# A spectral filter's second step, taken for two groups at a time on the four quarters of the matrix array

## The chip, the cores and the metric

The kernel runs on one core of a Trainium2 chip. The metric is the time of one execution on the device in microseconds (us). A core has TensorE (PE in the profile, with PEld for the loading of its weights), VectorE (DVE), ScalarE (ACT), GpSimd (POOL), SyncE (SP) and 16 DMA engines. Each engine takes its instructions in the order in which they are written; engines wait for each other through semaphores. Matmuls read SBUF and write PSUM, which DVE and ACT read; here POOL works on SBUF.

## The reference

Two layers, each a spectral filter A and then a token MLP B, both on a normalised input and added to it. x is 2048 x 640 in float32.

```python
def _A_ref(x, w_r, w_i):
    X = jnp.fft.rfft2(x, axes=(-2, -1))
    X = X * (w_r + 1j * w_i)
    return jnp.fft.irfft2(X, s=(S, D), axes=(-2, -1))

def _B_ref(x, w1, b1, w2, b2):
    h = _layernorm(x, axis=-1)
    u = _gelu(jnp.einsum("bsd,sf->bdf", h, w1) + b1)
    y = jnp.einsum("bdf,fs->bds", u, w2) + b2
    return y.transpose(0, 2, 1)

for layer in range(2):
    x = x + _A_ref(_layernorm(x), A_w_r, A_w_i)
    x = x + _B_ref(_layernorm(x), B_w1, B_b1, B_w2, B_b2)
```

## The kernel before

Transforms are matmuls with constant tables. To keep float32's precision at the speed of f16, an operand is split into a high and a low f16 part (names ending in h and l), and a product is three matmuls: high by high, high by low, low by high. The split is made by two engines: ACT writes the high part, DVE (or POOL) the rest.

The order of the program is `run` (L1371): in layer 1 it normalises, folds and takes the first matmul step over the 2048 rows, whose results are s1h and s1l; then `a1` (L408), the filter stage, which this case is about; `a2` (L675), the inverse's last steps; and the MLP (`b1st` L847, `b2nd` L1072), which runs `a1` and `a2` of layer 2 in between. `a1` sets `self.pin` (L574): from there each engine's order is the order of the text, through the helper at L48 that records nearly every operation. So the profile shows nearly everything at L49, and groups are told by their tiles.

`a1` works on 16 groups of the spectrum. One group passes through these steps:

- D, `dstage` (L481): 16 matmuls of 160 or 161 columns, the step over the 640 channels, from s1h, s1l, tables tD and a stacked rest (stk, by DMA through DRAM).
- ph and pl, `psplit` (L494): the split of D's result, 128 x 642, on ACT and DVE.
- S, `s2stage` (L517): the second step over rows, 12 matmuls of 128x128 weights (table tS2, half of it zeros) and 321 columns.
- ta and tb, `product` (L555): DVE multiplies S's result in PSUM by the filter's real and imaginary parts w (321 KB by DMA a group); POOL forms the complex product by two operations of 128 x 321.
- xh and xl, `xsplit` (L503), with the group's scale sx; `twice` (L511) copies 126 columns of each, on ACT and POOL.
- I, `is2stage` (L541): the inverse of S, 36 matmuls of 64x128 weights and 128 columns, two row halves at a time.
- Y, yt, Y2h, Y2l: `yevict` (L432) and `y2evict` (L447) on ACT read I's result; `y2split` (L452) on POOL casts yt to Y2h and forms the rest Y2l.

The loop (L584 to L632) runs these shifted: in the round of group g, PE runs D of g+1, I of g-3 and S of g; DVE takes ta and tb of g-1, pl of g+1, xl of g-2; ACT takes ph of g+1, xh of g-2, Y and yt of g-3. PSUM is a ring of four tiles of two banks, `big` (L89), used in the order of D, I, S. Between them stand extra steps: in layer 1 the scale of the filter (`scale_x` L215), of the MLP's bias (`scale_b` L234) and of its first weights (`scan1` L189, a sum of squares of 128 x 1024 on ACT, output junk; `scale1` L196); in both layers the split of the first weights (`wsplit` L823, tiles raw, wh and wl), in quarters of 128 x 512 over the last rounds. SP issues the loads of w, stk, raw and the inverse's tables tDi and tIM.

Of the kernel before, what the change touches and what calls it, by code (L numbers as in the profile page):

```python
# [33 lines left out]
YS = 2.0 ** -14  # L34
I32 = mybir.dt.int32
# [21 lines left out]
class Layers:  # L57
# [41 lines left out]
    def setup(self):  # L99
        nc, A = self.nc, self.A  # L100
        base = self.base = self.push("base", side="left")
        self.psum = self.push("ps", bufs=4, space=PSUM)
# [112 lines left out]
    def scale_x(self, pool):  # L215
# [5 lines left out]
        V.tensor_reduce(m, ps[:NG, 0, :128], op=ALU.max, axis=mybir.AxisListType.X)  # L221
# [3 lines left out]
        mm(ps[:, 1, :NG], b, self.eye[:NG, :NG], start=True, stop=True)  # L225
        yield
        q = pool.tile([128, NG], F32, name="xqq")
        V.tensor_scalar(q, ps[:, 1, :NG], SMALL, XS ** -2, op0=ALU.max, op1=ALU.mult)
# [5 lines left out]
    def scale_b(self):  # L234
# [6 lines left out]
        for ps in self.total(sq):  # L241
# [106 lines left out]
    def a0_s1h(self, j, pv, zs=ZS):  # L348
        self.T.activation(self.s1h[:, :, j], pv, AF.Copy, scale=S1S / (zs * TS))

    def a0_s1l(self, j, pv, zs=ZS):
        self.V.scalar_tensor_tensor(
            self.s1l[:, :, j], pv, S1S / (zs * TS), self.s1h[:, :, j], op0=ALU.mult, op1=ALU.subtract
        )

    def a0_tail(self, j, xt, pend):
# [24 lines left out]
        sc = S1S / (ZS * TS)  # L381
# [8 lines left out]
        for t0, t1 in pieces:  # L390
            ps = self.big()[:, 0]
            for t in range(t0, t1):
# [4 lines left out]
            T.activation(self.s1h[:, q, j], pv, AF.Copy, scale=sc)  # L397
            V.scalar_tensor_tensor(
                self.s1l[:, q, j], pv, sc, self.s1h[:, q, j], op0=ALU.mult, op1=ALU.subtract
            )  # L400
# [7 lines left out]
    def a1(self, first):  # L408
# [16 lines left out]
        yv = self.Y.rearrange("p a b j (g q c) -> p g q (a b j) c", q=2, c=4)  # L425
        y2 = [y.rearrange("p b j (g q c) -> p g q (b j) c", q=2, c=4) for y in self.Y2]
# [5 lines left out]
        def yevict(g, ps, lt=slice(0, 2)):  # L432
            T.activation(
                yv[:, g, :, lt.start * 32:lt.stop * 32], pairs(ps, lt.start * 128, lt.stop * 128), AF.Copy,
# [3 lines left out]
        def y2hi(g, ps):  # L438
            T.activation(y2[0][:, g], pairs(ps, 256, 384), AF.Copy, scale=YS)

        def y2lo(g, ps):
            for q in range(2):
                V.scalar_tensor_tensor(
                    y2[1][:, g, q], pairs(ps, 256, 384)[:, q], YS, y2[0][:, g, q], op0=ALU.mult, op1=ALU.subtract,
                )

        def y2evict(g, ps):  # L447
            yt = self.t(p, [128, 2, 32, 4], F32, "yt", 2)
# [23 lines left out]
        for q, a in zip(rest, (self.s1h, self.s1l)):  # L472
            nc.sync.dma_start(q.rearrange("c i g r -> (c i) g r"), a[:, 64:].rearrange("p g a b -> p g (a b)"))
        stack(G0)

        def wload(g):
            w = self.t(p, [128, 2, NL], F32, "w", 3)
# [3 lines left out]
        def dstage(g):  # L481
            ps = self.big()
            part = lambda t: tuple(s[:, t * 16 + g].rearrange("p a b -> p (a b)") for s in (self.s1h, self.s1l))
# [10 lines left out]
        def psplit(ps):  # L494
            ph = self.t(p, [128, 2, 322], F16, "ph", 2)
            pl = self.t(p, [128, 2, 322], F16, "pl", 2)
            sc = PQS / (S1S * TS)
            T.activation(ph[:, :, :NL], ps[:, :, :NL], AF.Copy, scale=sc)
            yield ph, pl
            V.scalar_tensor_tensor(pl[:, :, :NL], ps[:, :, :NL], sc, ph[:, :, :NL], op0=ALU.mult, op1=ALU.subtract)  # L500
            yield

        def xsplit(g, c, x):  # L503

            xh, xl = (q[:, :, c] for q in xs[g % 3])
            sc = self.sx[:, g:g + 1]
            i = T.activation(xh, x, AF.Identity, scale=sc)
            V.scalar_tensor_tensor(xl, x, sc, xh, op0=ALU.mult, op1=ALU.subtract)
            return i
# [6 lines left out]

        def s2stage(g, ph, pl):  # L517
            sp = 1 if g == 0 else 0
            ps = self.big()
            for ri in range(2):  # L520
                for q in range(2):
                    a = tuple(self.tS2[:, h, sp, 2 * ri + q] for h in range(2))
# [18 lines left out]
        def is2stage(g):  # L541
            ps = self.big()
# [12 lines left out]
        def product(ps, w):  # L555
            ta, tb = (self.t(p, [128, 2, NL], F32, a, n) for a, n in (("ta", 3), ("tb", 2)))
            V.tensor_tensor(ta, ps[:, :, :NL], w[:, 0:1].to_broadcast([128, 2, NL]), op=ALU.mult)
            V.tensor_tensor(tb, ps[:, :, :NL], w[:, 1:2].to_broadcast([128, 2, NL]), op=ALU.mult)
            G.tensor_tensor(ta[:, 0], ta[:, 0], tb[:, 1], op=ALU.subtract)
            return ta, G.tensor_tensor(ta[:, 1], tb[:, 0], ta[:, 1], op=ALU.add)  # L560

        def last_product(ps, w, tt, lt):

            c = slice(128 * lt, min(128 * lt + 128, NL))
            n = c.stop - c.start
            ta, tb = (q[:, :, c] for q in tt)
            V.tensor_tensor(ta, ps[:, :, c], w[:, 0:1, c].to_broadcast([128, 2, n]), op=ALU.mult)
            V.tensor_tensor(tb, ps[:, :, c], w[:, 1:2, c].to_broadcast([128, 2, n]), op=ALU.mult)
            V.tensor_tensor(ta[:, 0], ta[:, 0], tb[:, 1], op=ALU.subtract)
            G.tensor_tensor(ta[:, 1], tb[:, 0], ta[:, 1], op=ALU.add)  # L570

        quarter = lambda q: ((q // 2,), slice(q % 2 * 4, q % 2 * 4 + 4))

        self.pin = True  # L574
        w = {g: wload(g) for g in range(3)}
# [1078 lines left out]
```

## Time and profile before

| | us |
|---|---|
| median of 3 runs | 1044.95 (1043.96 to 1046.51) |
| the profiled execution | 1044.98 |
| its span, first to last instruction | 1043.2 |
| filter stage, layer 1: first S to the first table tDi | 63.43 to 136.47 |
| filter stage, layer 2: first S to the first table tDi | 576.49 to 646.41 |
| start of S to start of S in mid-stage, layer 2 | 599.46 to 603.46 |

The profile was taken on the only core, at a mean granted clock of 0.987. In the rows below, a start in us is followed by a duration, the engine, the line, the operation, its tiles out<-in with their shape and type, and, in brackets, the idle time just before and who ended it. A matmul row shows first the tile written (ps), then weights and moving operand, and x4 says that the row stands for four in a stretch. Engine rows of one operation overlap a little with the next one's, so what an operation costs its engine in a stream is the distance from its start to the next one's start.

### The profile page before, as it was taken

Reading aid. Unit: us, or ns where it says so; the run is one execution under the profiler, and the core shown is the slowest. Engines: PE = TensorE matmul, PEld = TensorE weight load, DVE = VectorE, ACT = ScalarE, POOL = GpSimd, SP = SyncE. Lnnn points to the kernel's source line nnn. Section 1 sums busy time; section 2 is a strip of 40 time slices with the busy share of each in tenths; the row PEclk is TensorE's granted clock in tenths of the full one; section 3 lists DMA queues with packets and bytes.
Section 4 is the critical chain, followed back from the end, with each engine's and each line's share of the span. In section 5 each row is a group of like instructions: output and inputs, shape, how many; then the busy total and the mean of one; then the engine's idle time right before and its main releaser. Section 6 shows DMA issues by size and latency. Waiting matters only on the chain.

```text
span 1043.2 us, 20923 instructions
## 1 busy us (share of the span) xinstructions
PE 998.0 (96%) x8315; PEld 733.2 (70%) x8315; DVE 710.4 (68%) x1437; ACT 585.3 (56%) x910; POOL 273.3 (26%) x482
## 2 busy tenths in 40 slices
PE   4889989999999999999997998999999999999998
PEld 3768766677777777777775786666777777777776
DVE  7978947854333956666675796677655564987885
ACT  5857669765555555555542475894644454634532
POOL 6928867300000002221112586770000000000000
PEclk9999989999999999999998998999999999999999
DMA  7864336532222264444424543455422232445511
GB/s 225 312 198 133 100 114 193 197 105 81 82 81 77 71 221 142 139 134 122 122 79 148 158 129 99 150 179 184 132 87 84 72 107 88 139 145 176 165 44 51
DMA packets 55305, 137.38 MB, mean 132 GB/s; under 512 B 6540, under 2 KB 12328, under 8 KB 55208
## 3 DMA queue, kind: packets, MB, share of 16 engines
q1 hardware_dynamic: 55208, 136.06, 41.2%
q8 instruction: 65, 1.06, 0.4%
q14 instruction: 32, 0.26, 0.1%
HBM read 112.96 MB, written 23.07 MB: 130 GB/s over the span
## 4 chain that ended last, share of the span: by engine, by line
PE 66%; DVE 16%; ACT 6%; POOL 5%; DMA 4%; issue 3%; SPq 1%; POOLq 0%; ACTq 0%; DVEq 0%
PE ps L49 66%; DVE wl L49 3%; DVE f L49 3%; POOL eo L49 2%; DMA xt<-x 2%; DVE st L49 2%; DVE s1l L49 2%; ACT wh L49 1%; ACT z L49 1%; DVE hl L49 1%; ACT junk L49 1%; ACT xt L49 1%; DVE xt L49 1%; DMA raw<-w 1%; DVE ta L49 1%
## 5 line engine op out<-in xcount | busy, mean ns | idle before, releaser
L49 PEld LDWEIGHTS <-wh 128*128 128x128 f16 x2992 | 290.1, 98 | 113.9 <-issue 2.0
L49 PEld LDWEIGHTS <-wl 128*128 128x128 f16 x1616 | 157.9, 98 | 61.9 <-DVE wl L49 0.5
L49 PE MATMUL ps<-hh,wh 128*128 128x320 f16 x896 | 186.3, 299 | 0.8 <-ACT hh L49 0.8
L49 PE MATMUL ps<-hl,wh 128*128 128x320 f16 x896 | 184.7, 299 | 0.0
L49 PE MATMUL ps<-hh,wl 128*128 128x320 f16 x832 | 171.5, 299 | 0.2 <-DVE wl L49 0.2
L49 DVE SCALAR_TENSOR_TENSOR wl<-raw,s,wh 128x1024 f16<-128x1024 f32 (+2 forms) x88 | 103.6, 1181 | 87.6 <-ACT wh L49 86.7
L49 PE MATMUL ps<-uh,wl 128*128 128x320 f16 x448 | 133.1, 299 | 0.0
L49 PE MATMUL ps<-ul,wh 128*128 128x320 f16 x448 | 133.1, 299 | 0.0
L49 ACT ACTIVATE wh<-raw,s 128x1024 f16<-128x1024 f32 (+2 forms) x92 | 94.8, 1048 | 68.0 <-PE ps L49 62.1
L49 PE MATMUL ps<-uh,wh 128*128 128x320 f16 x416 | 124.3, 299 | 0.0
L49 ACT ACTIVATE junk<-raw 128x896 bf16<-128x896 f32 (+1 forms) x60 | 59.6, 994 | 47.8 <-DMA raw<-w 47.8
L49 POOL TENSOR_TENSOR r<-v,mh 128x1 f32<-128x1 f32 x64 | 35.7, 559 | 141.3 <-DVE nm L49 129.0
L49 DVE TENSOR_TENSOR xt<-xt,ps 128x320 f32<-128x320 f32 (+1 forms) x96 | 44.9, 490 | 39.9 <-ACT ec L49 25.8
L49 PE MATMUL ps<-u,wo 128*128 128x320 f16 x504 | 69.9, 299 | 0.0
L49 DVE TENSOR_TENSOR f<-eo 128x256 f32<-128x256 f32 (+1 forms) x128 | 40.0, 365 | 41.9 <-POOL eo L49 41.3
L49 PEld LDWEIGHTS <-wo 128*128 128x128 f16 x504 | 49.3, 98 | 19.1
L49 ACT ACTIVATE z<-xt,nb,r 128x640 f32<-128x640 f32 x31 | 28.5, 919 | 55.8 <-POOL z L49 43.7
L49 DVE BATCH_NORM_STATS2 st<-xt 128x6 f32<-128x320 f32 x128 | 56.2, 481 | 5.0 <-DMA xt<-x 4.8
L49 PE MATMUL ps<-ph,tS 128*128 128x321 f16 (+2 forms) x288 | 59.1, 290 | 0.0
L49 POOL TENSOR_TENSOR eo<-z 128x320 f32<-128x320 f32 x63 | 54.2, 880 | 17.0 <-ACT z L49 15.1
L49 PE MATMUL ps<-tM,f 128*128 128x128 f32 x160 | 39.1, 420 | 19.4 <-DVE f L49 19.4
L49 PE MATMUL ps<-tDi,yh 128*128 128x322 f16 x256 | 55.9, 309 | 1.6 <-ACT yh L49 1.6
(166 smaller groups left out, 1907.5 us busy)
## 6 DMA issues: line engine op xcount, KB each, us to landing
raw<-w SPq DMA_DIRECT2D x56, 512.0 KB
xt<-x SPq DMA_DIRECT2D x80, 320.0 KB
w<-w SPq DMA_DIRECT2D x48, 321.0 KB
x<-xt SPq DMA_DIRECT2D x48, 320.0 KB
raw<-w SPq DMA_DIRECT2D x32, 448.0 KB
raw<-w2z SPq DMA_DIRECT2D x32, 448.0 KB
out<-xt SPq DMA_DIRECT2D x15, 320.0 KB
stk<-rest SPq DMA_DIRECT2D x42, 64.0 KB
```

The costliest lines, as they stand in the source:

```text
L49: i = f(*a, **k)
```

## The change

The table order of the second step is changed so that tS2's zeros make two blocks of 64x64 on the diagonal. Then two groups a = 2i and b = 2i+1 can share the array: `s2pair` runs, instead of 24 matmuls of 128x128, 48 of 64x64 on 321 columns, row half r going to its own PSUM tile and column half e holding group a or b. Each result tile thus holds half of both groups, and w, the scale's table (`gsel`) and the lanes of Y are dealt anew for the first 14 groups; groups 14 and 15 stay as they were. The first step's results lie in runs of four, not eight, and in layer 2 their low part is two DVE operations for one.

The loop goes over 8 pairs. The low parts pl are wanted only by the last third of S's matmuls. The scale sx moves from xsplit to DVE's ta and tb; xh becomes a plain copy, xl a subtraction, which for even groups is halved between DVE and POOL. Y2h is read from PSUM by ACT, and POOL keeps Y2l. PSUM's ring is three tiles and one that has its own tag ("one"), for the r = 1 half of a pair (and every fourth tile elsewhere). w has four buffers, not three. The extra steps move: `scale_x` behind pair 0, `scale_b` at i = 1 and 2, both scans at i = 2 with the reduce of their sums on DVE right behind, the rest of `scale1` at i = 3; they use spare columns of D's PSUM tile. The split of the first weights stands at i = 4 to 6 (high) and 4 to 7 (low).

Three places show how this moves instructions. The first is ACT in layer 1's filter stage, once the loop is full: before, one group's round,

```order
L49 ACTIVATE ph_1534<-ps_1517 128x2x321
L49 ACTIVATE xh_219_834<-ta_1495,sx 128x2x321
L49 ACTIVATE xh_219_834<-xh_219_834 128x2x63
L49 ACTIVATE Y_826<-ps_1537 128x2x64x4
L49 ACTIVATE yt_1602<-ps_1537 128x256
```

and with the change, one pair's round at the same place:

```order
L50 ACTIVATE ph_1572<-ps_1555 128x2x321
L50 ACTIVATE Y_826<-ps_1575 128x2x64x4
L50 ACTIVATE Y2h_827<-ps_1575 128x2x32x4
L50 ACTIVATE yt_1614<-ps_1575 128x256
L50 ACTIVATE ph_1644<-ps_1627 128x2x321
L50 ACTIVATE xh_219_834<-ta_1616 128x2x321
L50 ACTIVATE xh_219_834<-xh_219_834 128x2x63
L50 ACTIVATE xh_219_836<-ta_1693 128x2x321
L50 ACTIVATE xh_219_836<-xh_219_836 128x2x63
L50 ACTIVATE Y_826<-ps_1656 128x2x64x4
L50 ACTIVATE Y2h_827<-ps_1656 128x2x32x4
L50 ACTIVATE yt_1760<-ps_1656 128x256
```

Both xh of the pair now stand in a row ahead of the second Y, Y2h and yt, and these ahead of the next pair's ph.

The second is ACT in layer 1 around the scans of the first weights (junk). Before:

```order
L49 ACTIVATE yt_1319<-ps_1249 128x256
L49 ACTIVATE junk,sq_1325<-raw_1131 128x1024
L49 ACTIVATE ph_1344<-ps_1327 128x2x321
L49 ACTIVATE xh_219_836<-ta_1305,sx 128x2x321
L49 ACTIVATE xh_219_836<-xh_219_836 128x2x63
L49 ACTIVATE Y_826<-ps_1347 128x2x64x4
L49 ACTIVATE yt_1412<-ps_1347 128x256
L49 ACTIVATE junk,sq_1325<-raw_1133 128x1024
```

With the change:

```order
L50 ACTIVATE yt_1328<-ps_1224 128x256
L50 ACTIVATE junk,sq_1334<-raw_1112 128x1024
L50 ACTIVATE junk,sq_1334<-raw_1114 128x1024
L50 ACTIVATE ph_1356<-ps_1339 128x2x321
L50 ACTIVATE Y_826<-ps_1359 128x2x64x4
```

The two scans, which had a whole round between them, now stand one behind the other ahead of ph of group 6.

The third is DVE in layer 1 around the first wl, the low part of a quarter of the first weights. Before:

```order
L49 TENSOR_TENSOR ta_1780<-ps_1665,w_1511 128x642
L49 TENSOR_TENSOR tb_1781<-ps_1665,w_1511 128x642
L49 SCALAR_TENSOR_TENSOR pl_1728<-ps_1710,ph_1727 128x2x321
L49 SCALAR_TENSOR_TENSOR wl_1136<-raw_1131,s_72,wh_1135 128x512
L49 SCALAR_TENSOR_TENSOR xl_219_839<-ta_1684,sx,xh_219_838 128x2x321
```

With the change:

```order
L50 SCALAR_TENSOR_TENSOR pl_1645<-ps_1627,ph_1644 128x2x321
L50 TENSOR_TENSOR xl_219_835<-ta_1616,xh_219_834 128x321
L50 SCALAR_TENSOR_TENSOR wl_1117<-raw_1112,s_72,wh_1116 128x512
L50 SCALAR_TENSOR_TENSOR ta_1827<-ps_1702,sx,w_1406 128x642
L50 SCALAR_TENSOR_TENSOR tb_1828<-ps_1702,sx,w_1406 128x642
```

Before, wl came a round behind its wh and behind ta, tb and pl; now its wh is the last thing in the same round of ACT, and the next pair's ta and tb stand behind wl.

The diff, cut to what the prediction speaks of (of the loop only the new lines; the old one is in the kernel above):

```diff
-    def big(self):
+    def big(self, one=None):
+
+        if one is None:
+            self.turn += 1
+            one = self.turn % 4 == 0
+        tag, bufs = ("one", 1) if one else ("big", 3)
         self.n += 1
-        return self.psum.tile([128, 2, 512], F32, tag="big", name=f"ps{self.n}")
+        return self.psum.tile([128, 2, 512], F32, tag=tag, name=f"ps{self.n}", bufs=bufs)
...
-        ps = self.big()
-        mm(ps[:NG, 0, :128], self.xq, self.eye, start=True, stop=True)
+        mm(ps[:NG, 0, 384:], self.xq, self.eye, start=True, stop=True)
...
-        self.s1h = p.tile([128, 80, 16, 8], F16, name=f"s1h{self.n}")
-        self.s1l = p.tile([128, 80, 16, 8], F16, name=f"s1l{self.n}")
+        self.s1h = p.tile([128, 80, 2, 16, 4], F16, name=f"s1h{self.n}")
+        self.s1l = p.tile([128, 80, 2, 16, 4], F16, name=f"s1l{self.n}")
...
+        h, l = self.s1h[:, q, :, j], self.s1l[:, q, :, j]
+        if sc == 1.0:
+            self.V.tensor_tensor(l, pv, h, op=ALU.subtract)
+            return
+        for b in range(2):
+            self.V.scalar_tensor_tensor(
+                l[:, :, b], pv[:, :, b], sc, h[:, :, b], op0=ALU.mult, op1=ALU.subtract
+            )
...
+        def lanes(y, g):
+
+            if g < PG:
+                y = y.rearrange("p b j (u e q c) -> p u q e (b j) c", e=2, q=2, c=4)
+                return y[:, g // 2, g % 2]
+            return y.rearrange("p b j (g q c) -> p g q (b j) c", q=2, c=4)[:, g]
...
         def y2evict(g, ps):
+            y2hi(g, ps)
             yt = self.t(p, [128, 2, 32, 4], F32, "yt", 2)
             T.activation(yt, pairs(ps, 256, 384), AF.Copy, scale=YS)
             return yt
 
         def y2split(g, yt):
-            G.tensor_copy(y2[0][:, g], yt)
-            G.tensor_tensor(y2[1][:, g], yt, y2[0][:, g], op=ALU.subtract)
+            G.tensor_tensor(lanes(self.Y2[1], g), yt, lanes(self.Y2[0], g), op=ALU.subtract)
...
+        def xhi(g, c, x):
+            T.activation(xs[g % 3][0][:, :, c], x, AF.Copy)
+
+        def xlo(g, c, x, r=slice(0, 2), e=V):
+            xh, xl = (q[:, r, c] for q in xs[g % 3])
+            e.tensor_tensor(xl, x[:, r], xh, op=ALU.subtract)
 
...
+        def s2pair(u, x):
+
+            ps = self.big(False), self.big(True)
+            for a, b in ((0, 0), (1, 0), (0, 1)):
+                for ri in range(2):
+                    for q in range(2):
+                        for e in range(2):
+                            for r in range(2):
+                                m = slice(64 * r, 64 * r + 64)
+                                sp = 1 if u == e == r == 0 else 0
+                                mm(
+                                    ps[r][64 * e:64 * e + 64, ri, :NL], self.tS2[m, a, sp, 2 * ri + q, m],
+                                    x[e][b][m, q, :NL], start=a == b == q == 0, stop=b == q == 1,
+                                )
+            return ps
...
+        def times(o, ps, g, w, c=slice(0, NL)):
+            n = c.stop - c.start
+            V.scalar_tensor_tensor(
+                o, ps[:, :, c], self.sx[:, g:g + 1], w[:, c].unsqueeze(1).to_broadcast([128, 2, n]),
+                op0=ALU.mult, op1=ALU.mult,
+            )
+
+        def product(g, ps):
             ta, tb = (self.t(p, [128, 2, NL], F32, a, n) for a, n in (("ta", 3), ("tb", 2)))
-            V.tensor_tensor(ta, ps[:, :, :NL], w[:, 0:1].to_broadcast([128, 2, NL]), op=ALU.mult)
-            V.tensor_tensor(tb, ps[:, :, :NL], w[:, 1:2].to_broadcast([128, 2, NL]), op=ALU.mult)
+            times(ta, ps, g, w[g][:, 0])
+            times(tb, ps, g, w[g][:, 1])
             G.tensor_tensor(ta[:, 0], ta[:, 0], tb[:, 1], op=ALU.subtract)
-            return ta, G.tensor_tensor(ta[:, 1], tb[:, 0], ta[:, 1], op=ALU.add)
-
-        def last_product(ps, w, tt, lt):
-
-            c = slice(128 * lt, min(128 * lt + 128, NL))
-            n = c.stop - c.start
+            gi = G.tensor_tensor(ta[:, 1], tb[:, 0], ta[:, 1], op=ALU.add)
+            if g + 4 < NG:
+                w[g + 4] = wload(g + 4)
+            return ta, gi
...
+        def xbegin(g):
+            xh, _ = xs[g % 3]
+            xhi(g, whole, ta[g])
+            T.activation(xh[:, :, NL:], xh[:, :, 257:320], AF.Copy)
+
+        def xfinish(g):
+            x, (_, xl) = ta.pop(g), xs[g % 3]
+            if g % 2:
+                xlo(g, whole, x)
+            else:
+                xlo(g, whole, x, slice(1, 2), G)
+                xlo(g, whole, x, slice(0, 1))
+            G.tensor_copy(xl[:, :, NL:], xl[:, :, 257:320])
+
+        def evict(g):
+            yevict(g, pv[g])
+            yt[g] = y2evict(g, pv.pop(g))
+
+        last = NG // 2 - 1
+        for i in range(NG // 2):
+            a, b, k = 2 * i, 2 * i + 1, 2 * i - 4
+            pa = dstage(a)
+            pa = phi(pa) if i else pquarters(pa)
+            if k >= 0:
+                pv[k] = is2stage(k)
+                evict(k)
             if i:
+                x = product(a - 2, ps2.pop(a - 2))
+                if k >= 0:
+                    xfinish(k + 1)
+                ta[a - 2], _ = x
+                if k >= 0:
+                    y2split(k, yt.pop(k))
+            pb = d = dstage(b)
+            pb = phi(pb) if i else pquarters(pb)
+            stack(2 * i + 4)
+            if i:
+                pa = plo(*pa)
+                xbegin(a - 2)
+            if k >= 0:
+                pv[k + 1] = is2stage(k + 1)
+            if i == 1:
+                pb = plo(*pb)
+            if i:
+                ta[a - 1], gi = product(a - 1, ps2.pop(a - 1))
+                if i > 1:
+                    pb = plo(*pb)
+            if i < last:
+                ps2[a], ps2[b] = s2pair(i, (pa, pb))
+            else:
+                ps2[a] = s2stage(a, *pa)
+            if i == 2:
+                nc.sync.dma_start(self.tDi, A["tDi"])
+            if i in (3, 4):
+                c = slice((i - 3) * 8, (i - 3) * 8 + 8)
+                nc.sync.dma_start(self.tIM[:, c], A["tIM"][:, c])
+            if first and i == 0:
+                for _ in self.scale_x(p, d):
                     pass
+            if i:
+                xfinish(a - 2)
+                if i < last:
+                    xbegin(a - 1)
             if k >= 0:
+                evict(k + 1)
+                y2split(k + 1, yt.pop(k + 1))
+            if i == 1:
                 self.wload(0)
                 self.wopen(0)
+            if first:
+                at = lambda: d[:, 1, 400:401]
+                if i == 1:
+                    sb = self.scale_b(at)
+                if i in (1, 2):
+                    next(sb)
+                    next(sb)
+                if i == 2:
+                    self.scan1(0)
+                    sc0 = self.scale1(0, at)
+                    next(sc0)
+                if i == 3:
+                    next(sc0)
+                    next(sc0)
+            for q in {4: (0, 1), 5: (2,), 6: (3,)}.get(i, ()):
+                self.wsplit(0, quarter(q)[0], lo=False, part=quarter(q)[1])
+            if i > 3:
+                self.wsplit(0, quarter(i - 4)[0], hi=False, part=quarter(i - 4)[1])
...
-            r_in = j16 * 8 + c8
+            r_in = c8 // 4 * 64 + j16 * 4 + c8 % 4
...
+    half = out[:PG].reshape(PG // 2, 2, 2, 64)
+    out[:PG] = half.transpose(0, 2, 1, 3).reshape(PG, 128).copy()
```

More of the change, by code (lines that the diff above doesn't have):

```diff
@@ L101, in setup @@
         base = self.base = self.push("base", side="left")
-        self.psum = self.push("ps", bufs=4, space=PSUM)
+        self.psum = self.push("ps", bufs=1, space=PSUM)
+        self.turn = 0
         self.dram = self.push("dr", space=DRAM)
@@ L240, in scale_b @@
         yield
[L241 removed]
+        for ps in self.total(sq, at):
             yield
@@ L396, in a0_tail @@
             q = slice(t0 * 16, t1 * 16)
[L397 to L400, printed above, removed]
+            self.a0_s1h(j, pv, q=q)
+            self.a0_s1l(j, pv, q=q)
     def s1_all(self, j, fh, fl):
@@ L438, in y2hi @@
         def y2hi(g, ps):
-            T.activation(y2[0][:, g], pairs(ps, 256, 384), AF.Copy, scale=YS)
+            T.activation(lanes(self.Y2[0], g), pairs(ps, 256, 384), AF.Copy, scale=YS)
         def y2lo(g, ps):
@@ L481, in dstage @@
         def dstage(g):
-            ps = self.big()
-            part = lambda t: tuple(s[:, t * 16 + g].rearrange("p a b -> p (a b)") for s in (self.s1h, self.s1l))
+            ps = self.big(False)
+            part = lambda t: tuple(s[:, t * 16 + g].rearrange("p q a b -> p (q a b)") for s in (self.s1h, self.s1l))
             for c, bk, o0, o1, k in CL:
@@ L584, in a1 @@
-        for g in range(NG - 1):
-            q = psplit(dstage(g + 1))
-            pp[g + 1] = next(q)
-            if g > 2:
-                pv[g - 3] = is2stage(g - 3)
-            ps2[g] = s2stage(g, *pp.pop(g))
-            i = g % NC
-            if i:
-                stack(g + 3)
-            k = g - 1
-            if first and g == 0:
-                for _ in self.scale_x(p):
-                    pass
+        w = {g: wload(g) for g in range(4)}
+        ps2, pv, yt, ta = {}, {}, {}, {}
```

144 lines of the change are left out of this document (54 added, 90 removed).

## The prediction

> **What bounds the kernel now.** I read the page's busy times and chain of waits first, then the windows of the filter stage, then single rows in order of time. A fraction after a start is the time of the operation in microseconds; pitch is start to start.
>
> ```profile
> PE 998.0 (96%) x8315; PEld 733.2 (70%) x8315; DVE 710.4 (68%) x1437; ACT 585.3 (56%) x910; POOL 273.3 (26%) x482
> PE 66%; DVE 16%; ACT 6%; POOL 5%; DMA 4%; issue 3%; SPq 1%; POOLq 0%; ACTq 0%; DVEq 0%
> ```
>
> TensorE (PE) is the bound over the span, but the filter stage must be read by itself. Two windows of it in layer 2 (columns: span, PE, PEld, DVE, ACT and POOL busy, granted clock, DMA share, GB/s) and one early window of layer 1:
>
> ```profile
> 598.00:604.00 6.00, 6.00 (x110) 4.92 (x108) 5.13 (x8) 4.01 (x8) 4.79 (x9) 1.00 0.36 94
> 604.00:610.00 6.00, 6.00 (x87) 4.95 (x85) 5.23 (x7) 3.48 (x8) 5.27 (x8) 1.00 0.46 129
> 68.00:74.00 6.00, 5.89 (x43) 4.16 (x42) 4.51 (x7) 1.39 (x3) 1.80 (x3) 0.72 0.59 183
> ```
>
> PE has no gap, but DVE is at 5.2 and POOL at 5.0 of 6.0: every engine but ACT is nearly full, so time taken from PE alone need not come off the end. One group on PE, D (first step), I (inverse second step), S (second step), next D:
>
> ```profile
> 601.11 0.30 PE L49 MATMUL ps<-tD,s1h 128*128 128x160 f16 x2
> 602.35 0.29 PE L49 MATMUL ps<-tI,xh 64*128 64x128 f16 x4
> 603.46 0.31 PE L49 MATMUL ps<-ph,tS 128*128 128x321 f16 x1
> 605.12 0.31 PE L49 MATMUL ps<-tD,s1h 128*128 128x160 f16 x2
> ```
>
> D takes 602.35−601.11 = 1.24, I 1.11, S 1.66, a group 4.01. S is 12 matmuls of 321 columns, so 0.138 each. Two groups cost 8.02.
>
> **What PE is spared.** The 48 quarter matmuls of a pair, four at a time, are 12 passes of 0.138 = 1.66 for two groups instead of 3.32. D and I stay. I add 0.1 for changing the array's form: 2×1.24+2×1.11+1.66+0.1 = 6.46 a pair, 1.56 less. For the 14 pairs of both layers that is −21.8, the most that can be gained.
>
> **What else must turn once a pair.** The order of every engine is fixed, so a chain that comes back to its own start sets a period of its own. Rows for its steps (ACT, DVE, POOL):
>
> ```profile
> 602.46 0.71 ACT L49 ACTIVATE ph<-ps 128x642 f16<-128x642 f32 x1 [1.48 <-PE ps L49]
> 603.06 0.83 ACT L49 ACTIVATE xh<-ta,sx 128x642 f16<-128x642 f32 x1
> 603.92 0.31 ACT L49 ACTIVATE xh<-xh 128x126 f16<-128x126 f16 x1
> 604.13 0.58 ACT L49 ACTIVATE Y<-ps 128x512 f32<-128x512 f32 x1
> 604.61 0.38 ACT L49 ACTIVATE yt<-ps 128x256 f32<-128x256 f32 x1
> 616.89 0.72 ACT L49 ACTIVATE wh<-raw,s 128x512 f16<-128x512 f32 x1
> 650.82 0.62 ACT L49 ACTIVATE yh<-Y 128x512 f16<-128x512 f32 x1
> 603.20 0.83 DVE L49 SCALAR_TENSOR_TENSOR pl<-ps,ph 128x642 f16<-128x642 f32 x1 [0.32 <-ACT ph L49]
> 603.94 1.16 DVE L49 SCALAR_TENSOR_TENSOR xl<-ta,sx,xh 128x642 f16<-128x642 f32 x1
> 605.32 0.83 DVE L49 TENSOR_TENSOR ta<-ps,w 128x642 f32<-128x642 f32 x1 [0.22 <-PE ps L49]
> 606.06 0.81 DVE L49 TENSOR_TENSOR tb<-ps,w 128x642 f32<-128x642 f32 x1
> 602.96 0.75 POOL L49 TENSOR_TENSOR ta<-ta,tb 128x321 f32<-128x321 f32 x1 [0.57 <-DVE tb L49]
> 603.66 0.75 POOL L49 TENSOR_TENSOR ta<-tb,ta 128x321 f32<-128x321 f32 x1
> 605.43 0.73 POOL L49 TENSOR_TENSOR Y2l<-yt,Y2h 128x256 f16<-128x256 f32 x1
> ```
>
> In the new order (rows of ACT and DVE in the part on the change) ACT runs, per pair, ph(a), Y, Y2h, yt of group k, ph(b), xh and its copy of a−2, the same of a−1, then Y, Y2h, yt of k+1, then the next pair's ph. DVE runs ta and tb of a−2, a rest xl, pl(a), ta and tb of a−1, pl(b), xl. So the next ph(a) stands behind yt(k+1), that behind xh(a−1), that behind POOL's two operations on a−1, those behind tb(a−1), that behind pl(a), that behind ph(a). Step by step: ph to pl 0.74 (603.20−602.46); pl 0.74 (to 603.94); ta 0.74 (606.06−605.32); tb 0.90 (0.81 and a handover); POOL 0.70 (603.66−602.96) and 0.80; xh 0.76 (its 0.86 to the next start, less 0.1, since the plain copy at 650.82 is 0.62 against 0.72 with a scale at 616.89, and the scale has moved to DVE); copy 0.21; Y 0.48; Y2h and yt 0.28 each (from the 0.38 of yt, less the overlap that Y shows). Sum **6.63**. POOL may still be at Y2l when tb ends (0 to 0.45) and DVE's xl and a POOL operation get in each other's way (xl takes 1.16 above where pl of the same size takes 0.83): up to 0.3. So 6.63 to 7.4; I take **7.2** for a steady pair, since POOL's work per pair (four of 0.72, two of 0.73, half an xl, two copies) is 5.6 and it rarely stands free. It binds above PE's 6.46: of 1.56 a pair about half is left.
>
> **Layer 2, from start to end.** S starts that close the parts:
>
> ```profile
> 576.49 0.30 PE L49 MATMUL ps<-ph,tS 128*128 128x321 f16 x1
> 587.44 0.31 PE L49 MATMUL ps<-ph,tS 128*128 128x321 f16 x1
> 632.07 0.31 PE L49 MATMUL ps<-ph,tS 128*128 128x321 f16 x1
> 620.04 0.73 DVE L49 SCALAR_TENSOR_TENSOR wl<-raw,s,wh 128x512 f16<-128x512 f32 x1
> 620.70 1.38 DVE L49 SCALAR_TENSOR_TENSOR xl<-ta,sx,xh 128x642 f16<-128x642 f32 x1
> ```
>
> They are groups 0, 3 and 14. Group 3 ends at 587.44+1.66 = 589.10, and from there to group 14's start are 42.97. After: pair 0 must wait for group 1's ph and pl too, 1.3 after 576.49, and ends 3.0 after it. Pair 1's second PSUM tile is the one buffer of its kind, which tb(1) must have read: D(2), D(3) 2.48, ph(3) 0.75, pl(3) 0.74, ta and tb 1.55, S 1.66, handovers 0.2: 7.4, end at 586.9, **−2.2**. Then six periods to group 14, less its S: 6.5 (the loop is not full yet), 7.2, 7.2, 9.5, 7.85, 7.85, −1.66 = 44.4 against 42.97, **+1.5**. The 9.5: with i = 4 the first two wh (0.72 each, row 616.89) stand on ACT behind yt(k+1), and DVE's wl waits for the first, with the next ta and tb queued behind it, which otherwise lie beside Y and ph: 0.72+0.73+1.48 of DVE after yt, less 0.6 that ran on anyway: +2.3. The two later wl cost their wh's 0.65 each; before, wl took 0.73 (620.04) and xl grew to 1.38. The first split of this layer, now two operations, adds **+0.3**. Layer 2: −0.4.
>
> **Layer 1** adds the scale work:
>
> ```profile
> 63.43 0.30 PE L49 MATMUL ps<-ph,tS 128*128 128x321 f16 x1
> 71.17 0.47 PE L49 MATMUL ps<-pl,tS 128*128 128x321 f16 x1
> 77.12 0.31 PE L49 MATMUL ps<-ph,tS 128*128 128x321 f16 x1
> 122.13 0.31 PE L49 MATMUL ps<-ph,tS 128*128 128x321 f16 x1
> 86.54 1.06 ACT L49 ACTIVATE junk<-raw 128x1024 bf16<-128x1024 f32 x1
> 87.48 0.20 ACT L49 ACTIVATION_READ_ACCUMULATOR junk<-raw 128x1 f32 x1
> 88.12 0.71 ACT L49 ACTIVATE ph<-ps 128x642 f16<-128x642 f32 x1 [0.44 <-PE ps L49]
> 67.02 0.17 DVE L49 TENSOR_SCALAR sx<-qi 128x16 int32<-128x16 int32 x1
> ```
>
> Group 3 ends at 78.78; to group 14's start 43.35, 0.4 over layer 2. The start gains more here, since before one S ran at half clock (0.47 a matmul at 71.17, window at 0.72): −1.6 to −3.2, I take **−2.4**. Base as in layer 2 **+1.5**, less the 0.4. At i = 2 DVE's reduce for the bias waits on ACT behind xh: **+0.9**. Both scans of the first weights now stand together before ph(6): 2×(1.06+0.20) = 2.5 on the loop, and the reduce of their sums holds ta(4), tb(4) on DVE, which lose 1.2 of cover: **+3.7**; before, one scan at a time was hidden, ph at 88.12 still waited 0.44 for PE. At i = 3 and 4 the small scale operations (six of 0.17 with handovers, about 1.1) and D(8), whose buffer waits for yt(3) instead of running ahead (1.24, partly beside them): **+2.0**. At i = 4 some of the wh wait is then met already: **−0.6**. Layer 1: +4.7. If ACT's own slack, 7.2 less its 5.2 of work, took a scan, 3.7 becomes 1.2; if nothing is covered, 5.
>
> Outside the filter stage only the splits of the first step write in runs of four: ACT's copies keep their size, and layer 1's DVE split drops a scale; I put that at nothing, between the +0.3 above and as much less. Sum: +4.7−0.4 = +4.3 on the profiled run's 1044.98 (span 1043.2 and 1.8 around it), which is the median of the runs, 1044.95, to 0.03: 1049.3, said as **1049**. I allow 1045.5 to 1052 for this case.
>
> **Rivals.** (1) *The loop does not bind*: POOL is free when tb ends and handovers are shorter, so PE sets 6.46. Then six periods less S are 37.1, −5.9 a layer, the starts −3.1, the scale work and the wl waits partly covered (+3.7 of some 9): 2×−9.0+0.3+3.7 = −14, **1031**, on the other side of no change. For it: the loop's bare sum is only 0.17 over PE. Against: two thirds of its steps are measured without waits, and POOL was at 5.27 of 6.0.
> (2) *Weights of the quarters are not hidden.*
>
> ```profile
> L49 PEld LDWEIGHTS <-tS 128*128 128x128 f16 x204 | 17.2, 98 | 6.9
> L49 PE MATMUL ps<-tI,xh 64*128 64x128 f16 x380 | 18.8, 219 | 2.4 <-ACT Y L49 2.3 <-ACT xh L49 0.2
> ```
>
> A load takes 98 ns and lies under the other matmuls now, S being 0.138 a matmul all told. No row shows a load into half the columns while the other half computes. If 12 passes each pay 0.1, PE needs 7.66 a pair, 0.46 above the loop: 14×0.46 = +6.4, **1055**.
> The Trainium skill speaks for this in kind (TensorEngine Tiling (Array Packing), Restrictions: column tiling disables Fast Weight Load), and the Trainium skill's page TensorE: Matmul & The Clock Gate, LDWEIGHTS, prices a load at columns/1.2 ns, 53 ns for 64 columns; an estimate by them is 12×53 = 0.64 a pair, 7.10, still under the loop, which would leave 1049 and turn rival 1 into about 1040. No run here shows a column-tiled load.
> (3) *The quarters run two at a time*, so the change does not do what it says on PE: only row halves are shown side by side (I's 36 matmuls of 128 columns in 1.11 are 31 ns each, where 128 columns alone need 0.138×128/321 = 55). S of a pair would be 3.3 and PE 8.1, 0.9 above the loop: 12.6, less some 2 of waits that PE would then cover: **1060**.
> (4) *Layer 1's extra work falls into waits* that the loop leaves anyway: 3 less, **1046**.
>
> **Chances.** Forecast 0.48, rival 1 0.24, rival 2 0.11, rival 3 0.03, rival 4 0.14. A measurement of this kernel tells about 0.3% (3.1 us) from no change, so slower begins at 1048.1 and faster ends at 1041.8. Forecast: 0.36 slower, 0.12 within. Rival 1: 0.22 faster, 0.02 within. Rivals 2 and 3: slower. Rival 4: 0.11 within, 0.02 faster, 0.01 slower. Sums: 0.24, 0.25, 0.51. The range goes from 1034 (rival 1 with half its gain eaten) to 1056 (rival 2); outside are the better half of rival 1, 0.12, and rivals 2 and 3 at their worst, 0.06.
>
> **What would show it.** PE: S of a pair lasts about 1.7 (right) or 2.9 and 3.3 (rivals 2, 3); in the steady stretch of layer 2 pairs start 7.2 apart with PE idle about 0.7, released by ACT's yt or ph; 6.5 with PE full means rival 1. DVE's first wl follows a wait on wh, with a pair of 9 to 10. In layer 1 two scans stand ahead of ph(6) and that pair takes 10 or more; if it takes 8, rival 4. The forecast is wrong if the stage, first S to the first table of the inverse, is shorter than before by over 3 in either layer.

## The result, and the profile after

The changed kernel takes 1060.32 us (median of 4 runs, 1058.59 to 1061.05) against 1044.45 for the kernel before: 1.0146 times as long, 95% interval 1.0126 to 1.0166, 15.9 us more. The direction was forecast, the size was not: 1049, with a range up to 1056.

The profiled execution took 1060.71, its span is 1058.9, 15.7 over the span before. Busy times and chain of waits on the page of the changed kernel:

```profile
PE 988.4 (93%) x8651; PEld 728.1 (69%) x8651; DVE 703.6 (66%) x1456; ACT 593.2 (56%) x940; POOL 267.7 (25%) x468
PE 73%; DVE 8%; ACT 6%; POOL 6%; DMA 3%; issue 3%; SPq 0%; POOLq 0%; DVEq 0%; ACTq 0%
```

TensorE has 9.6 us less to do, and the kernel is longer. Where that went is seen by cutting both traces at the same four points: the first matmul of D and the first of the inverse's table tDi in each layer. Before (the tDi starts, 136.47 and 646.41, are in the table of the kernel before):

```profile
59.31 0.31 PE L49 MATMUL ps<-tD,s1h 128*128 128x160 f16 x2 [0.80 <-ACT s1h L49]
571.97 0.45 PE L49 MATMUL ps<-tD,s1h 128*128 128x160 f16 x2
```

After:

```profile
60.23 0.32 PE L50 MATMUL ps<-tD,s1h 128*128 128x160 f16 x2 [0.80 <-ACT s1h L50]
142.39 0.72 PE L50 MATMUL ps<-tDi,yh 128*128 128x322 f16 x2 [0.78 <-ACT yh L50]
584.42 0.45 PE L50 MATMUL ps<-tD,s1h 128*128 128x160 f16 x2
661.19 0.72 PE L50 MATMUL ps<-tDi,yh 128*128 128x322 f16 x2 [0.78 <-ACT yh L50]
```

| stretch | before | after | more | forecast |
|---|---|---|---|---|
| start to layer 1's first D | 59.31 | 60.23 | 0.9 | 0 |
| layer 1's filter stage, first D to tDi | 77.16 | 82.16 | 5.0 | 4.7 |
| from there to layer 2's first D (layer 1's MLP) | 435.50 | 442.03 | 6.5 | 0 |
| layer 2's filter stage | 74.44 | 76.77 | 2.3 | -0.4 |
| from there to the end | 396.8 | 397.7 | 0.9 | 0 |

The forecast's -0.4 holds 0.3 for layer 2's first split, which falls into the stretch above it. One trace gives such a stretch to 1 or 2 us: in e2, an experiment below whose filter stages are those of the kernel before, they take 75.0 and 73.6 instead of 77.2 and 74.4.

**The filter stage.** S of the pairs in layer 2, TensorE:

```profile
595.46 0.32 PE L50 MATMUL ps<-ph,tS 64*64 64x321 f16 x1
598.77 2.36 PE L50 MATMUL ps<-ph,tS 64*64 64x321 f16 x31 [3.00 <-DVE tb L50]
601.90 0.32 PE L50 MATMUL ps<-tD,s1h 128*128 128x160 f16 x2
606.62 1.48 PE L50 MATMUL ps<-ph,tS 64*64 64x321 f16 x32
614.21 1.30 PE L50 MATMUL ps<-ph,tS 64*64 64x321 f16 x32
615.99 0.31 PE L50 MATMUL ps<-tD,s1h 128*128 128x160 f16 x2
621.12 1.64 PE L50 MATMUL ps<-ph,tS 64*64 64x321 f16 x32
631.00 1.73 PE L50 MATMUL ps<-ph,tS 64*64 64x321 f16 x32
638.84 1.48 PE L50 MATMUL ps<-ph,tS 64*64 64x321 f16 x32
646.43 0.31 PE L50 MATMUL ps<-ph,tS 128*128 128x321 f16 x1
```

A pair's S takes 615.99−614.21 = 1.78: the quarters run four at a time and their weights are hidden. In the other steady pairs it takes 1.96 to 2.2, because the first matmul stands alone: the second is the first to write the one buffer of its kind, and that waits for DVE's tb of the pair before. The pair at 631.00 shows it (the second row is the timeline from 631.40 on):

```profile
630.51 0.88 DVE L50 SCALAR_TENSOR_TENSOR tb<-ps,sx,w 128x642 f32<-128x642 f32 x1
631.44 1.15 PE L50 MATMUL ps<-ph,tS 64*64 64x321 f16 x26
```

From the second matmul on, S takes 1.77 or 1.78 in each of these pairs. The periods are 7.6, 6.9, 9.9, 7.8, 7.6 where 7.2, 7.2, 9.5, 7.85, 7.85 were forecast, and TensorE stands up to 0.8 a pair for ACT's yt, as forecast. Who released it between 606 and 647 (us in total, times, longest):

```profile
PE ps L50 <- ACT yt L50: 3.7, 5, 0.8
```

Pair 1 waits 3.00 for tb, the reader of the one buffer.

In layer 1 (pair 1's end, pairs 2 and 3, group 14) the round with the two scans, before 93.73, takes 10.4:

```profile
78.00 0.45 PE L50 MATMUL ps<-tD,s1h 128*128 128x160 f16 x2
83.34 1.30 PE L50 MATMUL ps<-ph,tS 64*64 64x321 f16 x32
93.73 1.74 PE L50 MATMUL ps<-ph,tS 64*64 64x321 f16 x32
127.63 0.31 PE L50 MATMUL ps<-ph,tS 128*128 128x321 f16 x1
```

**Layer 1's MLP.** Apart from layer 2's first split nothing in its steps changed, yet TensorE stops at two matmuls on ones, which add up the squares of coming weights. After, and the same two matmuls before:

```profile
243.11 0.16 PE L50 MATMUL ps<-sqb,ones 128*128 128x1 bf16 x1 [1.10 <-ACT q L50]
432.36 0.16 PE L50 MATMUL ps<-sqb,ones 128*128 128x1 bf16 x1 [4.20 <-DVE xt L50]
```

```profile
235.37 0.17 PE L49 MATMUL ps<-sqb,ones 128*128 128x1 bf16 x1
420.25 0.17 PE L49 MATMUL ps<-sqb,ones 128*128 128x1 bf16 x1
```

The distance between the two traces grows from 6.5 to 7.7 at the first and from 7.7 to 12.1 at the second, and to 14.7 by the next one, since TensorE comes back at a low clock. Two windows of after, the idle one and the one behind it (the granted clock is the third number from the end):

```profile
428.00:432.00 4.00, 0.16 (x2) 0.00 (x0) 2.57 (x8) 2.95 (x5) 0.74 (x2) 0.87 0.23 77
432.00:436.00 4.00, 3.64 (x15) 2.11 (x15) 3.97 (x9) 1.82 (x3) 0.00 (x0) 0.50 0.56 174
```

### The profile page after: what moved, and what is told of

Its sections match the earlier page's. It is cut to its first block, busy times and chain, and to the rows that moved or that the text cites. A ratio compares the mean times of both kernels' runs of the same rounds, so it can differ in the third digit from the quotient of the medians.

```text
span 1058.9 us, 21657 instructions
## 1 busy us (share of the span) xinstructions
PE 988.4 (93%) x8651; PEld 728.1 (69%) x8651; DVE 703.6 (66%) x1456; ACT 593.2 (56%) x940; POOL 267.7 (25%) x468
## 3 DMA queue, kind: packets, MB, share of 16 engines
q8 instruction: 68, 1.11, 0.4%
## 4 chain that ended last, share of the span: by engine, by line
PE 73%; DVE 8%; ACT 6%; POOL 6%; DMA 3%; issue 3%; SPq 0%; POOLq 0%; DVEq 0%; ACTq 0%
PE ps L50 73%; POOL ta L50 3%; DVE f L50 2%; DMA raw<-w 2%; DMA xt<-x 1%; ACT xh L50 1%; DVE s1l L50 1%; DVE st L50 1%; POOL eo L50 1%; POOL Y2l L50 1%; ACT wh L50 1%; DVE tb L50 1%; ACT Y L50 1%; DVE ta L50 1%; ACT junk L50 1%
## 5 line engine op out<-in xcount | busy, mean ns | idle before, releaser
L50 DVE SCALAR_TENSOR_TENSOR wl<-raw,s,wh 128x1024 f16<-128x1024 f32 (+2 forms) x88 | 106.8, 1218 | 89.1 <-ACT wh L50 88.7
L50 ACT ACTIVATE wh<-raw,s 128x1024 f16<-128x1024 f32 (+2 forms) x92 | 94.6, 1049 | 69.1 <-PE ps L50 63.6
L50 PEld LDWEIGHTS ps<-tM,f 128*128 128x128 f32 x160 | 34.9, 314 | 24.3 <-DVE f L50 23.9
L50 PE MATMUL ps<-tD,s1h 128*128 128x160 f16 (+1 forms) x288 | 41.9, 242 | 9.8 <-DVE tb L50 5.2
```

Source lines behind the costliest of these rows:

```text
L50: i = f(*a, **k)
```

## The experiments

Each was timed against the kernel before on its own chip, in three rounds. The names e1 to e10 stand for them; "order" below is the order of an engine's instructions.

| | time, us | ratio to before, 95% interval |
|---|---|---|
| the change | 1060.32 | 1.0146 (1.0126 to 1.0166) |
| e1, one operation for the low split | 1059.96 | 1.0147 (1.0128 to 1.0167) |
| e2, before with two operations | 1043.26 | 0.9993 (0.9982 to 1.0004) |
| e3, evictions ahead of xh | 1053.85 | 1.0085 (1.0059 to 1.0112) |
| e4, three edits | 1046.46 | 1.0026 (1.0015 to 1.0036) |
| e5, a buffer of its own for the sums | 1056.72 | 1.0113 (1.0088 to 1.0138) |
| e6, before with the split ring | 1048.52 | 1.0035 (1.0022 to 1.0048) |
| e7, e4 and e5 | 1042.49 | 0.9984 (0.9969 to 0.9998) |
| e8, e7 and scans apart | 1040.20 | 0.9960 (0.9946 to 0.9974) |
| e9, e8 with full matmuls | 1054.47 | 1.0094 (1.0075 to 1.0113) |
| e10, e8 with the weights' split spread | 1042.93 | 0.9980 (0.9967 to 0.9993) |

### What stops TensorE in the MLP: the order of ACT, or the ring of PSUM

The MLP's order is not pinned, and the two operations that now write layer 2's s1l (0.87 together, 0.81 before) had led the scheduler to put, in each round of the MLP's last third, a scan of weights ahead of z on ACT. The scan waits for its load. That was the first theory.

```diff
-        for b in range(2):
-            self.V.scalar_tensor_tensor(
-                l[:, :, b], pv[:, :, b], sc, h[:, :, b], op0=ALU.mult, op1=ALU.subtract
-            )
+        l, pv, h = (t.rearrange("p a b c -> p (a b) c") for t in (l, pv, h))
+        self.V.scalar_tensor_tensor(l, pv, sc, h, op0=ALU.mult, op1=ALU.subtract)
```

> The changed kernel with the low part of layer 2's first-step split written by one operation of 128x160x4 instead of two of 128x80x4. Theory A (order): the two operations made the scheduler, which orders the unpinned MLP of layer 1, put the scan of the next weights ahead of z on ACT; the scan waits for its load, z and the chain behind it wait with it, TensorE stands 4.2 us and runs slow for 2.6 more. With one operation the old order is back: 7 us less, near 1053, no idle over 1 us on TensorE before a matmul on ones between 400 and 440. Theory B (late loads): the weights come late because the filter stage ended later; then nothing changes, 1060.

> The kernel before, with only the low part of layer 2's first-step split written by two operations of 128x80x4 instead of one of 128x80x8. Theory A (order): the scan goes ahead of z on ACT here too, and the kernel before loses 5 to 7 us, 1050 to 1052, with the filter stages as they were. Theory B (late loads): the loads come as before, the operations cost 0.1 each beside other work: 1045.

Theory A fell twice. In e1 ACT's order is the old one again and the stall is still there; in e2 the new order is in the kernel before and costs nothing. Both times are those of theory B, late loads, which stays until e5. The row of e1:

```profile
431.93 0.16 PE L50 MATMUL ps<-sqb,ones 128*128 128x1 bf16 x1 [4.16 <-DVE xt L50]
```

The releaser says more than the loads do: a matmul that writes 128x1 waits for DVE's xt because it is to write the buffer that xt reads. In the compiled program before, this matmul writes from 408 on the same buffer in every round, and waits for the reader of its own last result (a small DVE operation, also named q; the q of the first stall is an ACT operation). With the change it waits in two rounds of four for xt, which comes late in the round. The change had replaced the ring of four PSUM buffers by three and one for the whole kernel, with every fourth tile in the one. e5 gives the one buffer to the sums, and leaves the three to all others outside the filter stage; e6 splits the ring of the kernel before.

```diff
-        if one is None:
-            self.turn += 1
-            one = self.turn % 4 == 0
...
-        ps = at() if at else self.big()[:, 0, :n]
+        ps = at() if at else self.big(True)[:, 0, :n]
```

> The changed kernel with only the PSUM ring outside the filter stage altered: the tile of the matmul on ones, which sums the squares of the weights, takes the single buffer, every other tile one of the three. Theory E (ring): with every fourth tile in the single buffer, the matmul on ones came to reuse a buffer that a late DVE operation (xt) or ACT operation (q) frees; in the kernel before it waits for the reader of its own last result. Then both stalls go, 1.25 near 235 and 4.4 with 2.6 of low clock near 430, and the time is 1051 to 1053. If the loads of the weights are late for another reason (theory B), it stays at 1058 to 1060.

> The kernel before with only its ring of four PSUM tiles split into three and one, every fourth tile in the one. Theory E (ring): it gets the two stalls of the MLP, 1.2 and 4 to 7 us, 1050 to 1053, with TensorE waiting for DVE's xt at a matmul on ones near 425. Theory B: the order of buffers is the same as in a ring of four, nothing changes, 1044 to 1045.

The matmul on ones of the second stall in e5, and the one that stands in e6:

```profile
427.98 0.17 PE L50 MATMUL ps<-sqb,ones 128*128 128x1 bf16 x1
```

```profile
410.26 0.16 PE L49 MATMUL ps<-sqb,ones 128*128 128x1 bf16 x1 [2.73 <-DVE xt L49]
```

In e5 both stalls are gone: its matmuls on ones stay 7.7 behind those of the kernel before from 227 to the last one, where the change was 14.7 behind. In e6 the second stall appears, one round earlier, in a kernel that has nothing else of the change; the first one (near 235) does not. So the ring is the cause of the stalls, and theory B falls. The size was overrated in both expectations: e5 gains some 3.5 (1.0146 to 1.0113), not 8, and e6 loses 0.35%, some 4, not 6 to 9. Part of the delay is taken back at the end of the MLP: from the last matmul on ones to layer 2's first D the change needs 584.42−542.99 = 41.4, the kernel before 43.7 and e5 44.8; why is not shown. Of the 6.5 that this stretch grew, e5 gives back 4.3 (442.0 to 437.7), and the ring alone adds 2.4 in e6 (435.5 to 437.9). What makes the other 2.2 is open.

### What sets the period of a pair

The chain of waits of the changed kernel between 606 and 632, by line and one round of it in order of time:

```profile
by line: POOL ta L50 38.6%; POOL Y2l L50 14.0%; issue 12.7%; ACT xh L50 12.2%; ACT Y L50 5.6%; DVE tb L50 3.4%; ACT yt L50 3.2%; ACT Y2h L50 3.2%; POOL xl L50 2.7%; ACT wh L50 2.4%; DVE ta L50 2.3%; POOLq L50 0.3%; DVE wl L50 0.2%; DVEq L50
613.34 0.46 POOL Y2l L50
613.79 0.20 issue
613.99 1.46 POOL ta L50 x2
615.45 0.02 issue
615.48 0.75 ACT xh L50
616.25 0.31 ACT xh L50
616.56 0.49 ACT Y L50
617.05 0.27 ACT Y2h L50
617.32 0.28 ACT yt L50
617.60 0.07 issue
617.67 0.73 POOL Y2l L50
```

No step of it is TensorE. It is the forecast's loop in its second half (POOL's two operations, xh, copy, Y, Y2h, yt), but it closes over POOL, not over ph and DVE: Y2l waits for yt, and POOL's next product is queued behind Y2l. e3 takes Y, Y2h and yt out of it.

```diff
                 xfinish(a - 2)
-                if i < last:
-                    xbegin(a - 1)
             if k >= 0:
                 evict(k + 1)
                 y2split(k + 1, yt.pop(k + 1))
+            if 0 < i < last:
+                xbegin(a - 1)
```

> The changed kernel with the evictions of group k+1 (Y, Y2h, yt) put ahead of xh of group a-1 on ACT. Theory C (loop): the chain ph, pl, ta, tb, POOL, xh, copy, Y, Y2h, yt, ph sets the pair's period; without Y, Y2h, yt it is 5.6, and TensorE's 6.5 is the bound: steady pairs of layer 2 6.6 to 6.9 apart instead of 6.9 to 7.8, 3 to 4 us less in each layer, near 1053. Rival D (TensorE or POOL sets the period): pairs stay at 7.6 and the time at 1060.

Steady pairs of e3 in layer 2, and its chain of waits from 602 to 616:

```profile
601.79 1.48 PE L50 MATMUL ps<-ph,tS 64*64 64x321 f16 x32
608.48 1.46 PE L50 MATMUL ps<-ph,tS 64*64 64x321 f16 x32
615.14 1.47 PE L50 MATMUL ps<-ph,tS 64*64 64x321 f16 x32
```

```profile
by line: PE ps L50 61.7%; POOL ta L50 15.8%; DVE ta L50 6.3%; DVE tb L50 5.8%; issue 5.4%; POOL Y2l L50 4.9%; POOL xl L50 1.6%; POOLq L50 0.1%
```

Pairs are 6.7 apart, TensorE leads the chain, and each stage is 3.4 to 3.5 shorter (82.16 to 78.67, 76.77 to 73.36). So the evictions behind xh set the period. That the loop closes over POOL and not over ph is read from the chain of waits alone, since e3 opens both. Of the 6.7, TensorE's own work is 2×1.24+2×1.11+1.77 = 6.5; the other 0.2 is the second matmul of S, which still waits for tb.

### Several mended together

e4 is e1 and e3, and pair 1's start:

```diff
             stack(2 * i + 4)
+            if i == 1:
+                ta[a - 1], gi = product(a - 1, ps2.pop(a - 1))
             if i:
                 pa = plo(*pa)
...
-            if i == 1:
+            if i:
+                if i > 1:
+                    ta[a - 1], gi = product(a - 1, ps2.pop(a - 1))
                 pb = plo(*pb)
-            if i:
-                ta[a - 1], gi = product(a - 1, ps2.pop(a - 1))
-                if i > 1:
-                    pb = plo(*pb)
```

For pair 1 the second ta and tb stand ahead of pl of group a, with both pl behind them. e7 adds e5's edit.

> The changed kernel with three edits: one operation for the low split (as e1), evictions ahead of xh (as e3), and in the first round with a product, pair 1, both groups' ta and tb ahead of both pl on DVE, so that the one PSUM buffer of its kind is read earlier. By theories A and C the gains add, -7 and -7, and pair 1 ends 2 us earlier in each layer and with less time at a low clock: 1041 to 1043, faster than the kernel before. If either theory is wrong, 1047 or more.

> The kernel of e4 (one operation for the low split, evictions ahead of xh, pair 1's ta and tb ahead of pl) with the sum's tile in the single buffer as in e5. Theory E: e4 lost 1.5 near 235 and some 4.4 between 420 and 530, so 1040 to 1041, faster than the kernel before by 4. Theory B: 1046 as e4.

Layer 2's stage falls to 69.1 in e4 and 70.5 in e7, from 73.4 in e3: reading the one buffer earlier is worth some 3 to 4, more than the 2 expected. In layer 1 nothing is seen of it from D on (78.8 and 78.9 against 78.7), but there TensorE's clock was at half near the start in these two traces (0.72 granted from 59 to 65 in e4, 1.00 in e3); from the first S on, both take 73.0 against 74.5. e4 missed its 1041 to 1043 by 3.5 since the first theory in it was wrong; e7, which mends the ring too, is 4 below it, and missed its 1040 to 1041 by 1.5.

In layer 1 the price of the scans is seen on DVE in the changed kernel:

```profile
89.31 0.16 DVE L50 TENSOR_REDUCE sqb<-sq 128x1 bf16<-128x2 f32 x1 [3.81 <-ACT junk L50]
89.39 0.89 DVE L50 SCALAR_TENSOR_TENSOR ta<-ps,sx,w 128x642 f32<-128x642 f32 x1
90.19 0.88 DVE L50 SCALAR_TENSOR_TENSOR tb<-ps,sx,w 128x642 f32<-128x642 f32 x1
```

The reduce waits 3.81 for the second scan with ta and tb behind it, as forecast. e8 puts one scan in each of two rounds:

```diff
-                if i == 2:
-                    self.scan1(0)
+                if i in (2, 3):
+                    self.scan1(0, (i - 2,))
+                if i == 3:
                     sc0 = self.scale1(0, at)
                     next(sc0)
-                if i == 3:
+                if i == 4:
```

> The kernel of e7 with layer 1's two scans of the first weights put into two rounds again (i = 2 and 3, the reduce of their sums at i = 3, the scale at i = 4). By the prediction's price for the scans (3.7, of which the later wait for the scale takes some back) layer 1 ends 1.5 to 2 us earlier than in e7: 1038 to 1039. If the scans fall into waits anyway (rival 4), as e7.

Layer 1's stage falls from 78.9 to 76.4, somewhat more than expected, the time from 1042.49 to 1040.20, above the expected 1038 to 1039 as e7 was above its own. e8 is 0.4% faster than the kernel before: 0.9960, 0.9946 to 0.9974.

### What the quarters are worth

e9 puts full matmuls back into e8, in the same place of the same order:

```diff
-PG = 14
+PG = 0
...
-                            for r in range(2):
-                                m = slice(64 * r, 64 * r + 64)
-                                sp = 1 if u == e == r == 0 else 0
-                                mm(
-                                    ps[r][64 * e:64 * e + 64, ri, :NL], self.tS2[m, a, sp, 2 * ri + q, m],
-                                    x[e][b][m, q, :NL], start=a == b == q == 0, stop=b == q == 1,
-                                )
+                            sp = 1 if u == e == 0 else 0
+                            mm(
+                                ps[e][:, ri, :NL], self.tS2[:, a, sp, 2 * ri + q],
+                                x[e][b][:, q, :NL], start=a == b == q == 0, stop=b == q == 1,
+                            )
```

> The kernel of e8 with the second step of a pair as 24 full 128x128 matmuls (half of each table zeros, groups dealt as in the kernel before) instead of 48 quarters; the order of all engines as in e8. In e8 steady pairs of layer 2 stand 6.7 apart with TensorE full. If the quarters run four at a time, the full ones cost 1.5 a pair more: pairs 8.1 to 8.2 apart, 8 to 9 us more in layer 2, 6 to 8 in layer 1, 1054 to 1057. If the loop of the other engines set the pair's period in e8 too, pairs stay within 0.5 of 6.7 plus what TensorE lacks, and the time moves by less than 5.

Steady pairs of e8, and of e9:

```profile
597.27 1.47 PE L50 MATMUL ps<-ph,tS 64*64 64x321 f16 x32
603.95 1.47 PE L50 MATMUL ps<-ph,tS 64*64 64x321 f16 x32
```

```profile
601.72 2.38 PE L50 MATMUL ps<-ph,tS 128*128 128x321 f16 x16
609.73 2.37 PE L50 MATMUL ps<-ph,tS 128*128 128x321 f16 x16
```

8.0 a pair, as two groups of the kernel before, against 6.7; 14.3 us in all, of which the filter stages have 6.2 and 7.1. With the order mended the quarters give two thirds of the 21.8 that the prediction called the most; e9 itself is 10 slower than the kernel before: so much the rest of the change (the order of the pairs, the scale on DVE, the split PSUM) still costs, and the quarters have to earn that first.

### The long pair at i = 4

e10 changes e8 so that one high quarter of the first weights is split per round (`{4: (0,), 5: (1,), 6: (2,), 7: (3,)}`) and each low one stands behind pl(a) of the next round.

> The kernel of e8 with the split of the first weights spread: one high quarter a round from i = 4 to 7 (two stood at i = 4), and each low quarter behind the next round's first pl on DVE, so that no ta or tb stands behind a low part that waits for its high one. By the prediction's account of the long pair at i = 4 (the wait costs 2.3) that pair falls from 8.7 to 7, 2 us less in each layer, 1036. If the pair is long because ACT and DVE have that much more to do in these rounds, the time comes back in the next pairs, and the result is 1040 to 1041.

Pair 5 follows pair 4 by 6.9 instead of 8.7, and the next two rounds take 7.8 each instead of 7.1, TensorE waiting 0.79 for tb; layer 2's stage is 69.6 against 69.7, layer 1's 77.6 against 76.4. The first account falls: the wait is gone and nothing is gained. The second fits layer 2, where the work of DVE and ACT, moved, comes back; but the time is 1042.93, above its 1040 to 1041 too, and why layer 1 lost 1.2 was not studied.

## Why the prediction was too low

- **Right: the quarters.** S of a pair was put at 1.66 and takes 1.78. Rivals 2 (2.9) and 3 (3.3) fall with that row; that the kernel's time is the 1060 of rival 3 is chance. The Trainium skill's loss of Fast Weight Load under column tiling (TensorEngine Tiling (Array Packing), Restrictions) can cost a part of this 0.1 at most; no wait for a load is shown. What the prediction left out is a wait in S itself: 0.2 to 0.4 in four of the five steady pairs of layer 2, for tb to read the one buffer, which it had priced for pair 1 alone.
- **Right in period, not in the loop's path.** 7.2 was taken and 6.9 to 7.6 measured, since POOL and ACT's second half of the chain are in both; that it closes over Y2l and POOL's queue was not in the path that was summed, so the agreement is in part luck. The step "POOL may still be at Y2l when tb ends (0 to 0.45)" held the true mechanism as a correction. ta and tb with the scale cost DVE 0.80 to the next start (90.19−89.39), where the sum had 0.74.
- **Right: layer 1's extra work.** From pair 1's end at 78.00 to group 14's S at 127.63 are 49.6, against a sum of 50.5; the scans' round took 10.4. Rival 4, that they fall into waits, is refuted by the 3.81 above and by e8. The agreement of the whole stage (5.0 against 4.7) leans on one trace, though: the sum's −2.4 was taken from the half clock of the kernel before at 68 to 74 (0.72), and e2, with the same filter stage, has 1.00 there.
- **Mis-sized: layer 2's start.** It was to bring −2.2. Pair 1 ended 17.5 after the first D instead of 14.9: pair 0 ended 1.1 later, and pair 1's S, behind its wait, took 601.90−598.77 = 3.1 instead of 1.7, because TensorE's clock had fallen in the 3.00 of waiting. That is most of the 2.7 by which layer 2 was missed.
- **Wrong: "Outside the filter stage only the splits of the first step write in runs of four ... I put that at nothing".** This is the step that failed. The same change split the ring of PSUM for the whole kernel; that was in the diff and was priced nowhere. Layer 1's MLP grew by 6.5 of the 15.7. The ring made its two stalls: 4.3 of the 6.5 by e5, 2.4 by e6, 3.5 to 4 of the kernel's time. The other 2.2 in this stretch is open, and with it a part of the miss. The order of the unpinned MLP had changed as well, and that, which looked like the cause, cost nothing (e1, e2).
- **Rival 1**, that TensorE sets the period, was given 0.24; for steady pairs of layer 2 it becomes true, to 0.2, with one edit on ACT (e3).

The 0.9 at the start and the 0.9 at the end were not studied; in the other kernels' traces the first D stands between 58.8 and 60.9.

## What to carry to other kernels

When an engine's share of the work is cut, write down the closed chain through the other engines, in the order in which they are queued, and price it against what is left of the cut; here an eviction queued behind an operation that waited for GpSimd held half of the gain. A buffer pool that a change splits for one stage is split for every stage: list who now takes whose buffer, and when that one is freed, in all of them. And what was cut may not be worth more than the order around it costs: the quarters give 14 us, and the rest of the change took more than that until three waits in its order, and the stalls of the split ring, were removed.

## What the runs showed of the hardware

- Four matmuls of 64x64 weights, on four quarters of the array, run side by side: 48 of 321 columns in 1.78 us, 37 ns each, where one of 128x128 takes 138. Where such a stretch takes longer here, its second matmul starts late, released by the reader of its PSUM buffer.
- TensorE's clock falls after short waits: after 3.00 us of waiting a pair's S took 3.1 instead of 1.8, after 4.20 the granted clock was 0.50 for the next 4 us and another 2.6 us went. The Trainium skill (TensorE: Matmul & The Clock Gate, HAM oscillation) names idle gaps of over about 3.4 us; here 3.00, and 2.73 in e6 (the distance there grew by 1.4 more behind the stall), were enough. Windows around the two, of the change and of e6 (granted clock 0.80 and 0.72):

```profile
600.00:604.00 4.00, 4.00 (x81) 3.08 (x75) 1.99 (x3) 1.76 (x3) 1.71 (x4) 0.80 0.21 73
408.00:412.00 4.00, 1.74 (x8) 1.04 (x8) 2.86 (x5) 4.00 (x7) 0.00 (x0) 0.72 0.22 86
```
